# Merging the sums over taps of one chunk with the logits of the next into one run of narrow products

## Chip, cores, metric

One core of a Trainium2 chip. The metric is device time in microseconds, the median of several executions of a whole program.

## The reference, cut to what matters

A token-wise layer norm feeds two branches, and their results are joined as `x + s * silu(b)`.

```python
qkv = (xn @ wqkv) ...            # S = 2048 tokens, D = 512, 32 heads of 16
idx = pos[:, None] - 2 * arange(8)[None, :]           # 8 taps, 2 apart, looking back
logits = einsum("bhsd,bhswd->bhsw", q, k[idx]) * scale
o      = einsum("bhsw,bhswd->bhsd", softmax(logits), v[idx])
s      = o @ wo
b      = (gelu(xn' @ w_gate) * (xn' @ w_up)) @ w_down   # 512 -> 1792 -> 512
```

(In the kernel the second branch uses the same normalized x.) With only eight taps, attention is elementwise work: for each tap VectorE multiplies q by shifted k, and TensorE sums the 16 elements of a head with a matrix of ones that has only 32 columns. The same goes for values. These are the "narrow" products.

Of the kernel before, what the change touches and what calls it, by code (L numbers as in the profile page):

```python
# [8 lines left out]
ALU = mybir.AluOpType  # L9
AF = mybir.ActivationFunctionType  # L10
BF16 = mybir.dt.bfloat16
F32 = mybir.dt.float32

P = 128
H = 32
DH = 16
W = 8
DIL = 2
WL = 4
WH = 2  # L20
PAD = 16
TQ = 512
VW = TQ + WL * DIL
EPS = 1e-5
SCALE = DH ** -0.5
# [3 lines left out]
def kernel(  # L29
# [13 lines left out]
    nc = tc.nc  # L43
    B, S, D = A_x.shape
# [8 lines left out]
    def pool(name, bufs, **kw):  # L53
        return ctx.enter_context(tc.tile_pool(name=name, bufs=bufs, **kw))
# [2 lines left out]
    wts = pool("wts", 1)  # L57
    big = pool("big", 1)
    qp = pool("qp", 1)
    ep = pool("ep", 2)  # L60
    vap = pool("vap", 1)
    prod = pool("prod", 8)
    hp = pool("hp", 16)
    xtp = pool("xtp", 2)
    op = pool("op", 1)
    sm = pool("sm", 3)
    sm2 = pool("sm2", 2)
    sm4 = pool("sm4", 4)
    xnp = pool("xnp", 6)
# [83 lines left out]
            )  # L153

    xnT = {}
    k_sb = big.tile([P, NC, PAD + S], BF16, name="k_sb")
    nc.vector.memset(k_sb[:, :, 0:PAD], 0.0)
    stats = const.tile([P, NT, nc.vector.BN_STATS_DIM], F32, name="stats")
    mv = const.tile([P, NT, nc.vector.BN_AGGR_DIM], F32, name="mv")
    mhalf = const.tile([P, 1], F32, name="mhalf")  # L160
# [87 lines left out]
    def qkv(j, fo, i0=0, n=TQ, ps=None):  # L248
        which, c = divmod(fo, NC)
        if fo == 0 and i0 == 0:  # L250
            st[j]["q"] = qp.tile([P, NC, TQ], BF16, name="q_sb")
        if ps is None:
            ps = mm.tile([P, n], F32, name="qkv_ps", tag="mm")[:]
            project(ps, wqkv_sb, fo * P, j, i0, n)
        if which == 0:
            nc.scalar.activation(out=st[j]["q"][:, c, i0 : i0 + n], in_=ps, func=AF.Copy)  # L256
        elif which == 1:
            lo = PAD + j * TQ + i0
            nc.scalar.activation(out=k_sb[:, c, lo : lo + n], in_=ps, func=AF.Copy)  # L259
        else:  # L260
            vst = sm4.tile([P, TQ], BF16, name="vst")
            nc.scalar.activation(out=vst[:], in_=ps, func=AF.Copy)  # L262
            lo = PAD + j * TQ
            nc.sync.dma_start(out=vT[c * P : (c + 1) * P, lo : lo + TQ], in_=vst[:])

    def load_v(j, wls=range(WL)):

        if wls[0] == 0:
            st[j]["va"] = vap.tile([P, DH, VW], BF16, name="v_arr")
        va = st[j]["va"]  # L270
        for wl in wls:
            nc.sync.dma_start(
                out=va[H * wl : H * (wl + 1), :, :],
                in_=bass.AP(
                    tensor=vT.tensor,
                    offset=PAD + j * TQ - WL * DIL - DIL * wl,
                    ap=[[SV * DH, H], [SV, DH], [1, VW]],
                ),
            )

    def qk_product(j, w):
        pk = prod.tile([P, NC, TQ], BF16, name="pk", tag="prod")
        off = PAD + j * TQ - w * DIL
        nc.vector.tensor_tensor(  # L284
            out=pk[:], in0=st[j]["q"][:], in1=k_sb[:, :, off : off + TQ], op=ALU.mult
        )
        st[j]["pk"][w] = pk

    def logits(j):
        nc.scalar.preload_act_table(AF.Exp)  # L290
        L = att.tile([P, NC, TQ], F32, name="L_ps", tag="quad")
        for wh in range(WH):
            for c in range(NC):
                for wl in range(WL):
                    nc.tensor.matmul(  # L295
                        L[H * wl : H * (wl + 1), wh, :],
                        lhsT=dsum[:, c, :],
                        rhs=st[j]["pk"][WL * wh + wl][:, c, :],
                        start=(c == 0),
                        stop=(c == NC - 1),  # L300
                    )
        E = st[j]["E"] = ep.tile([P, WH, TQ], BF16, name="E")
        nc.scalar.activation(out=E[:], in_=L[:, 0:WH, :], func=AF.Exp, scale=SCALE)
        if j == 0:
            for w in range(1, W):
                wh, wl = divmod(w, WL)
                nc.gpsimd.memset(E[H * wl : H * (wl + 1), wh, 0 : w * DIL], 0.0)

    def denominators(j):

        E = st[j]["E"]
        den = mm.tile([P, P], F32, name="den_ps", tag="mm")
        for wh in range(WH):
            for q in range(4):
                nc.tensor.matmul(  # L315
                    den[H * q : H * (q + 1), :],
                    lhsT=hsum[:],
                    rhs=E[:, wh, q * P : (q + 1) * P],
                    start=(wh == 0),
                    stop=(wh == WH - 1),  # L320
                )
        rs = sm2.tile([P, P], BF16, name="rs")
        with nc.allow_low_precision(reason="as the softmax of the reference"):
            nc.vector.reciprocal(out=rs[:], in_=den[:])
        st[j]["rs"] = rs

    def store_reciprocals(j):
        nc.sync.dma_start(out=rs_d[j][:, :], in_=st[j]["rs"][:])
# [60 lines left out]
    def down(j, tt, cols):  # L389

        n = cols.stop - cols.start
        y = mm.tile([P, n], F32, name="y_ps", tag="mm")
        for fc in range(NF):
            nc.tensor.matmul(  # L394
                y[:],
                lhsT=st[j][fc][:, tt * P : (tt + 1) * P],
                rhs=wd_sb[:, fc, cols],
                start=(fc == 0),
                stop=(fc == NF - 1),
            )  # L400
        sl = sm.tile([P, n], BF16, name="sl")
        nc.scalar.activation(out=sl[:], in_=y[:], func=AF.Silu)  # L402
        return sl

# [21 lines left out]
    def at(key, fn, *args):  # L426
        side.setdefault(key, []).append((fn, args))

    def run(stage, j, i):
        for fn, args in side.get((stage, j, i), ()):  # L430
            fn(*args)

    for i in range(TPQ):
        at(("qkv", 0, i), normalize, TPQ + i)
        at(("glu", 0, 7 + i), moments, 2 * TPQ + i)
        if i < 2:
            at(("glu", 0, i), transpose, TPQ + i)
        at(("glu", 0, 8 + i), normalize, 2 * TPQ + i)
        at(("glu", 1, 0), transpose_by_dma, 2 * TPQ + i)
        at(("glu", 1, 10 + i), moments, 3 * TPQ + i)  # L440
        at(("qkv", 2, 2 * i), normalize, 3 * TPQ + i)
        at(("glu", 2, 0), transpose_by_dma, 3 * TPQ + i)

    for w in range(W):
        at(("glu", 0, w), qk_product, 0, w)
    at(("glu", 0, 9), logits, 0)
    for i in range(8):
        at(("glu", 0, 11 + i) if i < 3 else ("qkv", 1, (0, 1, 2, 4, 5)[i - 3]),
           av_product, 0, i // 2, i % 2)
    at(("qkv", 1, 8), denominators, 0)  # L450
    at(("qkv", 1, 8), av_sums, 0)
    at(("qkv", 1, 8), store_reciprocals, 0)
    at(("qkv", 1, 10), spread_reciprocals, 0)
    at(("down", 0, 0), divide, 0)

    for j in range(1, NJ):
        for w in range(W):
            at(("qkv", j, 9 + w) if w < 3 else ("down", j - 1, w // 3), qk_product, j, w)
        for i in range(TPQ):
            at(("down", j - 1, i), load_v, j, [i])  # L460
        at(("glu", j, 0), logits, j)
        for i in range(8):
            at(("glu", j, 2 + i), av_product, j, i // 2, i % 2)
        at(("glu", j, 11), denominators, j)
        at(("glu", j, 11), av_sums, j)
        at(("glu", j, 11), store_reciprocals, j)
        at(("glu", j, 11), spread_reciprocals, j)
        at(("qkv", j + 1, 6) if j + 1 < NJ else ("down", j, 0), divide, j)


    HT = TPQ // 2
# [41 lines left out]
    for j in range(NJ):  # L513
        for fc in range(NF):
            run("glu", j, fc)
            glu(j, fc)
        if j + 1 < NJ:
            for i in range(12):
                run("qkv", j + 1, i)
                qkv(j + 1, i)  # L520

        todo = []
        for tt in range(TPQ):
            run("down", j, tt)
            last = j * TPQ + tt == NT - 1
            for cols in (slice(0, D // 2), slice(D // 2, D)) if last else (slice(0, D),):
                sl = down(j, tt, cols)
                if todo:
                    finish(*todo.pop())
                if last:  # L530
                    finish(j, tt, cols, sl)
                else:
                    todo.append((j, tt, cols, sl))
        if todo:
            finish(*todo.pop())
# [1 line left out]
_INS = ['A_x', 'A_wqkv', 'A_wo', 'B_x', 'B_w_gate', 'B_w_up', 'B_w_down']  # L537
_OUTS = [((1, 2048, 512), 'bfloat16')]
# [25 lines left out]
```

## The kernel before: what the change and the argument touch

Four chunks j of 512 tokens. For each chunk a gate-and-up stage (`glu`, 14 tiles), the q, k, v projections of the *next* chunk (`qkv`, 12 tiles), and a `down` stage (4 tiles of 128 tokens). Attention is hung into these stages by `at(stage, function)`, which runs the function ahead of that tile.

```python
k_sb = big.tile([P, NC, PAD + S], BF16)          # k of all chunks
prod, hp, ep, vap, att, mm = pools of 8, 16, 2, 1, 1, 4 buffers   # att, mm in PSUM

def qk_product(j, w):                            # one tap, 128 x 2048, VectorE
    nc.vector.tensor_tensor(out=pk, in0=q, in1=k_sb[:, :, off : off + TQ], op=mult)

def logits(j):                                   # narrow: 32 products of 32 columns
    L = att.tile([P, NC, TQ], F32, tag="quad")
    for wh, c, wl: nc.tensor.matmul(L[32*wl : 32*(wl+1), wh], lhsT=dsum[:, c], rhs=pk[4*wh+wl][:, c])
    E = exp(L)                                   # ScalarE, one activation of 1024

def denominators(j): ...                         # narrow: 8 products, then reciprocal on VectorE
def av_sums(j):      ...                         # narrow: 32 products into att "quad"

for j in range(1, NJ):
    qk_product(j, w)  at qkv j, tiles 9 to 11, and down j-1
    load_v(j, part)   at down j-1, one part per tile
    logits(j)         at glu j, tile 0
    av_product(j, .)  at glu j, tiles 2 to 9
    denominators(j), av_sums(j), store and spread reciprocals   at glu j, tile 11
    divide(j)         at qkv j+1, tile 6
# down(tt) and finish(tt - 1), the output product, alternate
```

(Loops written in one line and positions in prose are cuts of this text.)

The softmax here doesn't subtract the row's maximum and nothing guards it: scores larger than these inputs give would overflow.

## Time and profile before

| | before |
|---|---|
| device time, median | 229.72 us (3 runs, 229.64 to 230.14) |
| span of the trace, first to last instruction | 228.0 us |
| TensorE / VectorE / ScalarE busy | 98% / 65% / 57% |
| narrow runs | 8 |

### The profile page before, as it was taken

Reading aid. Unit: us, or ns where it says so; the run is one execution under the profiler, and the core shown is the slowest. Engines: PE = TensorE matmul, PEld = TensorE weight load, DVE = VectorE, ACT = ScalarE, POOL = GpSimd, SP = SyncE. Lnnn points to the kernel's source line nnn. Section 1 sums busy time; section 2 is a strip of 40 time slices with the busy share of each in tenths; the row PEclk is TensorE's granted clock in tenths of the full one; section 3 lists DMA queues with packets and bytes.
Section 4 is the critical chain, followed back from the end, with each engine's and each line's share of the span. In section 5 each row is a group of like instructions: output and inputs, shape, how many; then the busy total and the mean of one; then the engine's idle time right before and its main releaser. Section 6 shows DMA issues by size and latency. Waiting matters only on the chain.

```text
span 228.0 us, 3495 instructions
## 1 busy us (share of the span) xinstructions
PE 222.4 (98%) x1300; PEld 106.8 (47%) x1320; DVE 147.6 (65%) x234; ACT 129.8 (57%) x213; POOL 12.8 (6%) x44
## 2 busy tenths in 40 slices
PE   8999999999999999999999999999999999999993
PEld 6864444444444444444444444444444444444453
DVE  4585996999496298865945369735476429943324
ACT  3779769774423876467621686746642387647210
POOL 1046023100000000110000000000000000000000
PEclk9999999999999999999999999999999999999999
DMA  6999589971399211110287511110149700001011
GB/s 166 354 372 372 146 169 197 247 202 38 101 195 206 70 25 29 26 29 0 92 169 168 139 30 23 26 35 5 39 119 206 169 27 3 0 6 26 0 45 48
DMA packets 31264, 24.62 MB, mean 108 GB/s; under 512 B 10896, under 2 KB 31248, under 8 KB 31248
## 3 DMA queue, kind: packets, MB, share of 16 engines
q1 hardware_dynamic: 31248, 24.41, 42.8%
q8 instruction: 10, 0.16, 0.3%
q14 instruction: 6, 0.05, 0.1%
HBM read 18.74 MB, written 4.34 MB: 101 GB/s over the span
## 4 chain that ended last, share of the span: by engine, by line
PE 95%; ACT 2%; issue 1%; DVE 0%; ACTq 0%; DVEq 0%
PE u_ps L238 21%; PE y_ps L394 21%; PE g_ps L238 19%; PE qkv_ps L238 17%; PE s_ps L410 6%; PE L_ps L295 3%; PE o_ps L357 3%; PE warm_ps L220 2%; PE q_ps L238 1%; ACT u L384 1%; ACT L382 1%; PE tr L203 1%; PE den_ps L315 0%; ACT xnT L212 0%; ACT ge L382 0%
## 5 line engine op out<-in xcount | busy, mean ns | idle before, releaser
L238 PE MATMUL u_ps<-xnT,wu_sb 128*128 128x512 bf16 x224 | 57.5, 379 | 0.3
L238 PE MATMUL g_ps<-xnT,wg_sb 128*128 128x512 bf16 x213 | 56.3, 379 | 0.4
L394 PE MATMUL y_ps<-wd_sb,h 128*128 128x512 bf16 (+1 forms) x236 | 50.2, 366 | 0.1
L386 DVE TENSOR_TENSOR h<-ge,u 128x512 bf16<-128x512 bf16 x56 | 23.7, 424 | 37.0 <-ACT u L384 36.6
L284 DVE TENSOR_TENSOR pk<-q_sb,k_sb 128x2048 bf16<-128x2048 bf16 x32 | 37.5, 1216 | 7.0 <-ACT k_sb L259 7.0
L382 ACT ACTIVATE ge<-g_ps 128x512 bf16<-128x512 f32 x56 | 33.5, 598 | 14.9 <-PE g_ps L238 13.8
L384 ACT ACTIVATE u<-u_ps 128x512 bf16<-128x512 f32 x56 | 33.5, 598 | 14.7 <-PE u_ps L238 14.7
L238 PE MATMUL qkv_ps<-xnT,wqkv_sb 128*128 128x512 bf16 (+1 forms) x203 | 40.5, 354 | 0.3
L343 DVE TENSOR_TENSOR pv<-E,v_arr 128x2048 bf16<-128x2048 bf16 x32 | 38.6, 1218 | 0.2 <-issue 0.2
L394 PEld LDWEIGHTS <-h 128*128 128x128 bf16 x238 | 23.3, 98 | 25.3
L238 PEld LDWEIGHTS <-wu_sb 128*128 128x128 bf16 x224 | 21.9, 98 | 26.6 <-issue 0.3
L238 PEld LDWEIGHTS <-wg_sb 128*128 128x128 bf16 x224 | 21.3, 98 | 27.3 <-issue 3.0
L402 ACT ACTIVATE sl<-y_ps 128x512 bf16<-128x512 f32 (+1 forms) x17 | 9.7, 572 | 41.4 <-PE y_ps L394 39.0
L238 PEld LDWEIGHTS <-wqkv_sb 128*128 128x128 bf16 x224 | 21.8, 98 | 19.8 <-issue 0.4
L418 DVE TENSOR_TENSOR m<-s_ps,sl 128x512 bf16<-128x512 f32 (+1 forms) x17 | 11.2, 657 | 22.2 <-PE s_ps L410 22.2
L410 PE MATMUL s_ps<-wo_sb,oT 128*128 128x512 bf16 (+1 forms) x66 | 15.8, 366 | 0.2
L262 ACT ACTIVATE vst<-qkv_ps 128x512 bf16<-128x512 f32 x16 | 9.6, 598 | 6.5 <-PE qkv_ps L238 6.5
L188 POOL TENSOR_TENSOR rstd<-rstd,mhalf 128x1 f32<-128x1 f32 x12 | 7.7, 640 | 87.4 <-DVE rstd L185 87.4
L259 ACT ACTIVATE k_sb<-qkv_ps 128x512 bf16<-128x512 f32 (+1 forms) x20 | 10.2, 516 | 3.5 <-PE qkv_ps L238 3.2
L369 DVE TENSOR_TENSOR oT<-o_ps,rb 128x1024 bf16<-128x1024 f32 x8 | 9.4, 1216 | 3.1 <-DMA rb<-rs_d 3.1
L256 ACT ACTIVATE q_sb<-qkv_ps 128x512 bf16<-128x512 f32 (+1 forms) x16 | 8.7, 544 | 3.2 <-PE qkv_ps L238 3.0
L410 PEld LDWEIGHTS <-oT 128*128 128x128 bf16 x68 | 6.7, 98 | 7.2
(46 smaller groups left out, 105.9 us busy)
## 6 DMA issues: line engine op xcount, KB each, us to landing
v_arr<-vT SPq DMA_DIRECT2D x16, 520.0 KB, 5.4
vT<-vst SPq DMA_DIRECT2D x16, 128.0 KB, 1.8
out_dram<-o_t SPq DMA_DIRECT2D x15, 128.0 KB, 1.8
wg_sb<-in_B_w_gate_dram SPq DMA_DIRECT2D x2, 896.0 KB, 10.7
wu_sb<-in_B_w_up_dram SPq DMA_DIRECT2D x2, 896.0 KB, 12.3
wd_sb<-in_B_w_down_dram SPq DMA_DIRECT2D x1, 1792.0 KB, 12.3
wqkv_sb<-in_A_wqkv_dram SPq DMA_DIRECT2D x3, 512.0 KB, 5.2
x_sb<-in_A_x_dram SPq DMA_DIRECT2D x3, 512.0 KB, 11.6
```

Of the source, the lines that this page charges most:

```text
L238: nc.tensor.matmul(ps, lhsT=w[:, dk, lo : lo + P], rhs=xnT[j][:, dk, i0 : i0 + n], start=(dk == 0), stop=(dk == NC - 1),)
L259: nc.scalar.activation(out=k_sb[:, c, lo : lo + n], in_=ps, func=AF.Copy)
L262: nc.scalar.activation(out=vst[:], in_=ps, func=AF.Copy)
L284: nc.vector.tensor_tensor(out=pk[:], in0=st[j]["q"][:], in1=k_sb[:, :, off : off + TQ], op=ALU.mult)
L343: nc.vector.tensor_tensor(out=pv[:], in0=st[j]["E"][:, wh, :].unsqueeze(1).to_broadcast([P, 4, TQ]), in1=st[j]["va"][:, 4 * g : 4 * g + 4, ...
L382: nc.scalar.activation(out=ge[:], in_=g_ps[:], func=AF.Gelu_apprx_tanh)
L384: nc.scalar.activation(out=u[:], in_=u_ps[:], func=AF.Copy)
L386: nc.vector.tensor_tensor(out=h[:], in0=ge[:], in1=u[:], op=ALU.mult)
L394: nc.tensor.matmul(y[:], lhsT=st[j][fc][:, tt * P : (tt + 1) * P], rhs=wd_sb[:, fc, cols], start=(fc == 0), stop=(fc == NF - 1),)
L402: nc.scalar.activation(out=sl[:], in_=y[:], func=AF.Silu)
L410: nc.tensor.matmul(s[:], lhsT=st[j]["oT"][:, g, tt * P : (tt + 1) * P], rhs=wo_sb[:, g, cols], start=(g == 0), stop=(g == NC - 1),)
L418: nc.vector.tensor_tensor(out=m[:], in0=s[:], in1=sl[:], op=ALU.mult)
```

## The change

Its intent: sums of chunk j and logits of chunk j+1 use the array in the same narrow form, so put them side by side and switch forms fewer times. For that the products of q and k have to be ready earlier, the logits need other PSUM buffers (they move from the four-bank `quad` to two of the `mm` buffers), and room has to be found in SBUF: k is kept as two chunk buffers with a copied halo (the last 16 columns of the chunk before, to which the taps look back), and four of the eight products lie in v's buffer while v is not loaded. The core of the diff:

```diff
-    prod = pool("prod", 8)
-    hp = pool("hp", 16)
+    prod = pool("prod", 12)
+    hp = pool("hp", 14)
-    k_sb = big.tile([P, NC, PAD + S], BF16, name="k_sb")
+    k_sb = {0: kp.tile([P, NC, PAD + TQ], BF16, name="k_sb")}
...
+    def k_halo(j):
+        k_sb[j] = kp.tile([P, NC, PAD + TQ], BF16, name="k_sb")
+        nc.gpsimd.tensor_copy(out=k_sb[j][:, :, 0:PAD], in_=k_sb[j - 1][:, :, TQ : TQ + PAD])
+
+    def qk_products(j, ws, c0, n):              # n of the 4 column groups, from c0
+        for w in ws:
+            if w not in st[j]["pk"]:
+                if j and w >= WL:
+                    if w == WL:
+                        st[j]["pk4"] = vap.tile([P, WL, NC, TQ], BF16, name="pk4", tag="va")
...
     def logits(j):
+            L = [mm.tile([P, TQ], F32, name="L_ps", tag="mm")[:] for _ in range(WH)]
...
-        at(("glu", 0, 7 + i), moments, 2 * TPQ + i)
+        at(("down", 0, 1), moments, 2 * TPQ + i)
-        at(("glu", 0, 8 + i), normalize, 2 * TPQ + i)
+        at(("down", 0, 2), normalize, 2 * TPQ + i)
...
+    def sums(j):
+        if j + 1 < NJ:
+            nc.scalar.preload_act_table(AF.Exp)
+        denominators(j)
+        av_sums(j)
+        if j + 1 < NJ:
+            logits(j + 1)
+        reciprocals(j)
+        store_reciprocals(j)
+        spread_reciprocals(j)
+        if j + 1 < NJ:
+            load_v(j + 1)
     for j in range(1, NJ):
+        at(("qkv", j, 2), k_halo, j)
+        for i in range(2):
+            at(("qkv", j, 4 + 4 * i), qk_products, j, range(W), 2 * i, 2)
         for i in range(8):
-            at(("glu", j, 2 + i), av_product, j, i // 2, i % 2)
+            at(("glu", j, 3 + i), av_product, j, i // 2, i % 2)
+    at(("glu", NJ - 1, 12), sums, NJ - 1)
...
+            for i, fo in enumerate((0, 1, 4, 5, 2, 3, 6, 7, 8, 9, 10, 11)):
                 run("qkv", j + 1, i)
-                qkv(j + 1, i)
+                qkv(j + 1, fo)
+            for tt in range(TPQ):
+                run("down", j, tt)
+                sl.append(down(j, tt, full))
+                if tt == 0:
+                    sums(j)
+            divide(j)
+            for tt in range(TPQ):
+                finish(j, tt, full, sl[tt])
```

The five value products of chunk 0 that were spread over qkv tiles 0 to 5 are now all asked for at qkv tile 0. The last chunk, which has no next one, keeps its sums in its gate-and-up stage.

More of the change, by code (lines that the diff above doesn't have):

```diff
@@ L59 @@
     qp = pool("qp", 1)
-    ep = pool("ep", 2)
+    kp = pool("kp", 2)
+    ep = pool("ep", 1)
     vap = pool("vap", 1)
-    prod = pool("prod", 8)
-    hp = pool("hp", 16)
+    prod = pool("prod", 12)
+    hp = pool("hp", 14)
     xtp = pool("xtp", 2)
@@ L66 @@
     sm = pool("sm", 3)
+    slp = pool("slp", 4)
     sm2 = pool("sm2", 2)
@@ L155 @@
     xnT = {}
-    k_sb = big.tile([P, NC, PAD + S], BF16, name="k_sb")
-    nc.vector.memset(k_sb[:, :, 0:PAD], 0.0)
+    k_sb = {0: kp.tile([P, NC, PAD + TQ], BF16, name="k_sb")}
+    nc.vector.memset(k_sb[0][:, :, 0:PAD], 0.0)
     stats = const.tile([P, NT, nc.vector.BN_STATS_DIM], F32, name="stats")
@@ L257, in qkv @@
         elif which == 1:
-            lo = PAD + j * TQ + i0
-            nc.scalar.activation(out=k_sb[:, c, lo : lo + n], in_=ps, func=AF.Copy)
+            lo = PAD + i0
+            nc.scalar.activation(out=k_sb[j][:, c, lo : lo + n], in_=ps, func=AF.Copy)
         else:
@@ L268, in load_v @@
         if wls[0] == 0:
-            st[j]["va"] = vap.tile([P, DH, VW], BF16, name="v_arr")
+            st[j]["va"] = vap.tile([P, DH, VW], BF16, name="v_arr", tag="va")
         va = st[j]["va"]
@@ L279, in load_v @@
             )
-    def qk_product(j, w):
-        pk = prod.tile([P, NC, TQ], BF16, name="pk", tag="prod")
-        off = PAD + j * TQ - w * DIL
-        nc.vector.tensor_tensor(
-            out=pk[:], in0=st[j]["q"][:], in1=k_sb[:, :, off : off + TQ], op=ALU.mult
-        )
-        st[j]["pk"][w] = pk
-    def logits(j):
-        nc.scalar.preload_act_table(AF.Exp)
-        L = att.tile([P, NC, TQ], F32, name="L_ps", tag="quad")
+    def k_halo(j):
[7 more added lines that the diff above has]
+                        st[j]["pk4"] = vap.tile([P, WL, NC, TQ], BF16, name="pk4", tag="va")
+                    st[j]["pk"][w] = st[j]["pk4"][:, w - WL]
+                else:
+                    st[j]["pk"][w] = prod.tile([P, NC, TQ], BF16, name="pk", tag="prod")
+            off = PAD - w * DIL
+            nc.vector.tensor_tensor(
+                out=st[j]["pk"][w][:, c0 : c0 + n, :],
+                in0=st[j]["q"][:, c0 : c0 + n, :],
+                in1=k_sb[j][:, c0 : c0 + n, off : off + TQ],
+                op=ALU.mult,
+            )
+    def logits(j):
+        if j == 0:
+            nc.scalar.preload_act_table(AF.Exp)
+            quad = att.tile([P, NC, TQ], F32, name="L_ps", tag="quad")
+            L = [quad[:, wh, :] for wh in range(WH)]
+        else:
+            L = [mm.tile([P, TQ], F32, name="L_ps", tag="mm")[:] for _ in range(WH)]
+        E = st[j]["E"] = ep.tile([P, WH, TQ], BF16, name="E")
         for wh in range(WH):
@@ L295, in logits @@
                     nc.tensor.matmul(
-                        L[H * wl : H * (wl + 1), wh, :],
+                        L[wh][H * wl : H * (wl + 1), :],
                         lhsT=dsum[:, c, :],
@@ L301, in logits @@
                     )
-        E = st[j]["E"] = ep.tile([P, WH, TQ], BF16, name="E")
-        nc.scalar.activation(out=E[:], in_=L[:, 0:WH, :], func=AF.Exp, scale=SCALE)
+        for wh in range(WH):
+            nc.scalar.activation(out=E[:, wh, :], in_=L[wh], func=AF.Exp, scale=SCALE)
         if j == 0:
@@ L321, in denominators, with reciprocals @@
                 )
+        st[j]["den"] = den
+    def reciprocals(j):
+        den = st[j]["den"]
         rs = sm2.tile([P, P], BF16, name="rs")
@@ L400, in down @@
             )
-        sl = sm.tile([P, n], BF16, name="sl")
+        sl = slp.tile([P, n], BF16, name="sl")
         nc.scalar.activation(out=sl[:], in_=y[:], func=AF.Silu)
@@ L434 @@
         at(("qkv", 0, i), normalize, TPQ + i)
-        at(("glu", 0, 7 + i), moments, 2 * TPQ + i)
+        at(("down", 0, 1), moments, 2 * TPQ + i)
         if i < 2:
             at(("glu", 0, i), transpose, TPQ + i)
-        at(("glu", 0, 8 + i), normalize, 2 * TPQ + i)
+        at(("down", 0, 2), normalize, 2 * TPQ + i)
         at(("glu", 1, 0), transpose_by_dma, 2 * TPQ + i)
         at(("glu", 1, 10 + i), moments, 3 * TPQ + i)
-        at(("qkv", 2, 2 * i), normalize, 3 * TPQ + i)
+        at(("qkv", 2, i), normalize, 3 * TPQ + i)
@@ L442 @@
         at(("glu", 2, 0), transpose_by_dma, 3 * TPQ + i)
     for w in range(W):
-        at(("glu", 0, w), qk_product, 0, w)
+        at(("glu", 0, w), qk_products, 0, [w], 0, NC)
     at(("glu", 0, 9), logits, 0)
     for i in range(8):
-        at(("glu", 0, 11 + i) if i < 3 else ("qkv", 1, (0, 1, 2, 4, 5)[i - 3]),
-           av_product, 0, i // 2, i % 2)
-    at(("qkv", 1, 8), denominators, 0)
-    at(("qkv", 1, 8), av_sums, 0)
-    at(("qkv", 1, 8), store_reciprocals, 0)
-    at(("qkv", 1, 10), spread_reciprocals, 0)
@@ L454 @@
-    at(("down", 0, 0), divide, 0)
-    for j in range(1, NJ):
-        for w in range(W):
-            at(("qkv", j, 9 + w) if w < 3 else ("down", j - 1, w // 3), qk_product, j, w)
-        for i in range(TPQ):
-            at(("down", j - 1, i), load_v, j, [i])
-        at(("glu", j, 0), logits, j)
-        for i in range(8):
-            at(("glu", j, 2 + i), av_product, j, i // 2, i % 2)
-        at(("glu", j, 11), denominators, j)
-        at(("glu", j, 11), av_sums, j)
-        at(("glu", j, 11), store_reciprocals, j)
-        at(("glu", j, 11), spread_reciprocals, j)
-        at(("qkv", j + 1, 6) if j + 1 < NJ else ("down", j, 0), divide, j)
+        at(("glu", 0, 11 + i) if i < 3 else ("qkv", 1, 0), av_product, 0, i // 2, i % 2)
@@ new lines, in sums @@
+    def sums(j):
+        if j + 1 < NJ:
+            nc.scalar.preload_act_table(AF.Exp)
+        denominators(j)
[7 more added lines that the diff above has]
+            load_v(j + 1)
+    for j in range(1, NJ):
+        at(("qkv", j, 2), k_halo, j)
+        for i in range(2):
+            at(("qkv", j, 4 + 4 * i), qk_products, j, range(W), 2 * i, 2)
+        for i in range(8):
+            at(("glu", j, 3 + i), av_product, j, i // 2, i % 2)
@@ L517 @@
         if j + 1 < NJ:
-            for i in range(12):
+            for i, fo in enumerate((0, 1, 4, 5, 2, 3, 6, 7, 8, 9, 10, 11)):
                 run("qkv", j + 1, i)
-                qkv(j + 1, i)
-        todo = []
-        for tt in range(TPQ):
-            run("down", j, tt)
-            last = j * TPQ + tt == NT - 1
-            for cols in (slice(0, D // 2), slice(D // 2, D)) if last else (slice(0, D),):
-                sl = down(j, tt, cols)
-                if todo:
-                    finish(*todo.pop())
-                if last:
-                    finish(j, tt, cols, sl)
-                else:
-                    todo.append((j, tt, cols, sl))
-        if todo:
-            finish(*todo.pop())
+                qkv(j + 1, fo)
+            full = slice(0, D)
+            sl = []
+            for tt in range(TPQ):
[6 more added lines that the diff above has]
+                finish(j, tt, full, sl[tt])
+        else:
+            full, half = slice(0, D), (slice(0, D // 2), slice(D // 2, D))
+            sl = [down(j, tt, full) for tt in range(TPQ - 1)]
+            divide(j)
+            finish(j, 0, full, sl[0])
+            finish(j, 1, full, sl[1])
+            sl3 = down(j, 3, half[0])
+            finish(j, 2, full, sl[2])
+            finish(j, 3, half[0], sl3)
+            sl3 = down(j, 3, half[1])
+            finish(j, 3, half[1], sl3)
 _INS = ['A_x', 'A_wqkv', 'A_wo', 'B_x', 'B_w_gate', 'B_w_up', 'B_w_down']
```

## The prediction

> **What bounds the kernel now.** I read the page's busy shares and chain first, then the groups by form of TensorE, then the timelines of TensorE, VectorE and the DMA queue around one chunk boundary.
>
> ```profile
> span 228.0 us, 3495 instructions
> PE 222.4 (98%) x1300; PEld 106.8 (47%) x1320; DVE 147.6 (65%) x234; ACT 129.8 (57%) x213; POOL 12.8 (6%) x44
> ...
> PE 95%; ACT 2%; issue 1%; DVE 0%; ACTq 0%; DVEq 0%
> ```
>
> The chain is TensorE from end to end. A busy 98% could still hide gaps, since matmul ends are modelled, so I counted starts. Four 128x512 products of one projection start every 0.863 us in the timeline, 0.216 us each. From the first up product of chunk 1 (75.31) to that of chunk 2 (129.38) it is 54.07 us. Work in it: 28x4 gate and up, 48 qkv, 56 down, 16 output products, 232 x 0.2158 = 50.07; 64 narrow products, four at once, 16 x 0.2158 = 3.45; eight narrow ones of 128 columns, 0.11. That sums to 53.63. Only 0.44 us of the period is not work: TensorE does not wait for anybody in the middle. What the 0.44 is shows at the edges of a narrow run:
>
> ```profile
> 70.77 1.89 PE L410 MATMUL s_ps<-wo_sb,oT 128*128 128x512 bf16 x8
> 72.59 1.91 PE L295 MATMUL L_ps<-pk,dsum 128*32 128x512 bf16 x32
> 74.43 1.04 PE L238 MATMUL g_ps<-xnT,wg_sb 128*128 128x512 bf16 x3
> ```
>
> The columns are start, length, engine, line, operation. Eight wide products from 70.77 take 1.73 and end their slots at 72.49; the narrow run starts at 72.59. Its 32 products take eight slots, to 74.32; the next wide one starts at 74.43. So entering costs 0.10 us and leaving 0.11 us, 0.21 us a run. Two runs a chunk make the 0.44.
>
> **What the Trainium skill says.** TensorEngine Tiling (Array Packing), section Key Properties: "Changing tiling mode (not just tile) drains the TensorE". The trace agrees: 0.10 us at each edge, and no gap between the denominators and the value sums, both 32 columns wide. TensorE: Matmul & The Clock Gate, section "Wait — 56ns, not 53.3ns?", gives 215.7 ns from start to start for 512 columns warm; the trace has 0.216. The same page, section The mechanism (Part 3), says matmuls start and end in program order, without reordering; so one product that waits for data holds all behind it. No row before shows this, as none waits. ScalarE: Activation LUTs, section What ACT_TABLE_LOAD costs, has 1283 ns for a load plus a drain of about 1380 ns; the trace agrees with 1283 ns, but starts the load within 0.01 us of the activation before it ending, so I count no drain.
>
> **The change, part by part.**
>
> 1. Narrow runs. Before there are eight: logits and sums for each of four chunks. After, in program order, five: logits 0, sums 0 with logits 1, sums 1 with logits 2, sums 2 with logits 3, sums 3. Three runs fewer at 0.21 us: **-0.65 us**, all on the path. TensorE's instruction count is unchanged.
>
> 2. q k products in two halves. A 128x2048 product has a pitch of 1.136 us (five in 5.76 with the last one's tail), a 128x512 one 0.335 (h at 43.58, next at 43.91). The line through both gives 0.60 us for 128x1024, so eight w in two halves take 16 x 0.602 = 9.63 against 9.09: VectorE pays 0.5 us a chunk. It has 35% idle; what counts is when the last half ends against when the merged run wants it. The logits now come about 15 us after the first qkv product; before they came at the end of the down stage, about 28 us after.
>
> 3. That deadline in chunk 1. Here five value products of chunk 0 stand in front:
>
> ```profile
> 42.44 1.22 DVE L343 TENSOR_TENSOR pv<-E,v_arr 128x2048 bf16<-128x2048 bf16 x1
> ...
> 46.85 5.76 DVE L343 TENSOR_TENSOR pv<-E,v_arr 128x2048 bf16<-128x2048 bf16 x5
> 52.53 0.95 DVE L324 RECIPROCAL rs<-den_ps 128x128 bf16<-128x128 f32 x1
> ```
>
> The moments and normalizations that stood in front of these move away, but the fourth load of v lands at 42.06, so the series can start only some 0.3 us earlier, and ends near 52.25. Then the halves: first halves of all eight w to 57.1, second halves of w 0 to 3 to 59.5, of w 4 to 7 to 61.9. TensorE: qkv starts at 44.54 as before; 48 slots to 54.90, one down tile (14 slots) to 57.92, entry 0.10, denominators 0.11, value sums 1.73: logits of w 0 to 3 start at 59.86, in time. Those of w 4 to 7 start at 60.72, their third c group at 61.15, and its w 7 needs the last half, ready at about 62.0. TensorE stops: **+0.9 us**. In chunks 2 and 3 nothing stands in front: k's second column group is there some 4.2 us after the first qkv product, the halves end by 14, and the group that needs the last one comes at 16.6. No stop there.
>
> 4. Transposes by DMA. The sixteen for chunk 2 are issued after the output writes of chunk 0:
>
> ```profile
> 73.08 1.40 SPq L421 DMA_DIRECT2D out_dram<-o_t  x2
> 74.58 21.68 SPq L230 DMA_TRANSPOSE xnT<-xn  x16
> ...
> 128.66 21.10 SPq L230 DMA_TRANSPOSE xnT<-xn  x16
> ```
>
> Issue alone takes 21 us, and the last lands 22.8 us after the first is issued (97.40), 22.2 for chunk 3 (150.87). qkv of chunk 2 started at 100.67, so there was a slack of over 3 us. It goes from both ends. The sums leave the glu stage, so glu to qkv shrinks to 28 x 0.8635 = 24.2 us. And the four output products now come in one piece at the end: m waits 1.13 us after the first one starts, then m and o_t have a pitch of 1.07, so the fourth o_t ends 5.5 us after the first starts, 2.0 after the glu stage has begun; with the write's issue the transposes start at 2.5. The last lands at 2.5 + 22.8 = 25.3; the first projection wants its fourth piece at 24.2 + 0.65 = 24.8: **+0.5 us** for chunk 2. With 22.2 it is 24.7 for chunk 3: nothing.
>
> 5. v's buffer is lent to four products. Its loads can start only after the merged logits, and the queue has reciprocals to store and spread first: for chunk 1 at about 66.3. Four loads in a row took 5.7 us for the first and 14 to the last (issue 27.98, last landed 42.06), so 80.4. The first value product comes after h of the third glu tile, about 6.4 us into the stage, near 81.5. In time, by 1 us; later by 3 or more.
>
> 6. Small things. ScalarE gains a table load a chunk (1.28 us) and eight short activations in place of four long ones; at 57% busy and with waits of about 3 us before each silu, free. GpSimd copies three halos. Divide for chunk 0 ends near 70.4, its first reader comes at 71.7.
>
> Sum: -0.65 + 0.9 + 0.5 = **+0.7 us** on 229.72: **230.4 us**, an increase of 0.3%.
>
> **Rivals.** (a) Only the drains count: both waits fit in slack that I cut too fine. 229.1 us. For it: the two waits are differences of about 1 us between sums of 15 to 25 us, and VectorE's starting point rests on one landing time. Against: both are series of fixed durations, which agree to a few hundredths in all chunks of the trace. (b) The transposes are late in both chunks, or the v loads, now four at once and then output writes in the same rings, push them or the first value products back by 1 to 3 us: 231 to 233 us. For it: in chunk 0 transposes issued behind four v loads landed 11.8 us later. Against: by the time they are issued most of v has landed. (c) VectorE's late series delays the reciprocals, their spreading and so the division: TensorE would wait at the first output product, 1 us or more, 231.5. For it: chunk 0's moments and normalizations, about 5 us, now stand between. Against: my count leaves 1.3 us.
>
> **Range and chances.** All of a merged drain is 0.65 us, and nothing else in the change removes TensorE work, so under 229 is hardly to be had; the low end, 228.9, is rival (a) with run-to-run room. The high end, 231.4, is the sum with one more us of rivals (b) or (c). Two per cent is 4.6 us: faster is out of reach of the mechanism, slower would need several of the waits at once. Faster 0.005, same 0.98, slower 0.015.
>
> **What would show it.** In the timeline of the changed kernel: five narrow runs with 0.1 us at each edge and no gap between value sums and logits within one; a stop of 0.5 to 1.3 us inside the first merged run, before products of pk's last w, put down to VectorE, and none in the two others; a stop of up to 1 us at the first projection of chunk 2, with the sixteenth transpose landing just before it, and less at chunk 3; m and o_t in blocks of four. The chain of waits should have VectorE or DMA pieces at just these two places. I am wrong if TensorE's idle time elsewhere is over 0.5 us, if either stop is absent, or if the period between chunks 2 and 3 does not fall by about 0.2 us.

## More of the kernel before

One more line, of the groups by cost, is used later. It ends with the busy time, the mean of one in ns, and the idle time just before them.

```profile
L343 DVE TENSOR_TENSOR pv<-E,v_arr 128x2048 bf16<-128x2048 bf16 x32 | 38.6, 1218 | 0.2 <-issue 0.2
```

The value products (`pv`) waited for nothing: the loads of v were in time. And TensorE, in the view of waits, waited twice, both at the start of the program:

```profile
PE warm_ps L220 <- PEq L548: 0.8, 1, 0.8
PE q_ps L238 <- ACT xnT L212: 0.2, 1, 0.2
```

## The result, and the profile after

Ratios here and below are the mean time of one kernel's runs over that of the other's in the same rounds, so not quite the ratio of the medians quoted.

| | before | after | ratio, 95% interval |
|---|---|---|---|
| first measurement | 229.73 us (229.47 to 230.14, 6 runs) | 231.25 us (230.57 to 231.99, 6 runs) | 1.0064 [1.0043, 1.0085] |
| again, in a later job | 229.92 us (229.65 to 230.90, 11 runs) | 230.91 us (230.70 to 231.07, 6 runs) | 1.0033 [1.0015, 1.0051] |

The change costs 0.3 to 0.6%. The page's head and the chain's shares by engine:

```profile
span 229.1 us, 3573 instructions
...
PE 223.6 (98%) x1320; PEld 107.0 (47%) x1320; DVE 149.1 (65%) x258; ACT 135.0 (59%) x220; POOL 13.8 (6%) x47
...
PE 71%; DMA 11%; DVE 8%; SPq 7%; issue 1%; DVEq 0%
```

TensorE's busy share is as before, 98%: that number does not tell a wait of one or two microseconds. (1320 against 1300 products is no change; some records were missing from the trace of before.) The chain of work that ended last, followed back from the last instruction, gives a hint (no proof; see late_run): it left TensorE. Followed in order of time (start, length, what), it goes through a load of v and VectorE before it comes back to TensorE in the middle of the first merged run:

```profile
30.20 12.34 DMA v_arr<-vT
...
49.46 3.48 DVE pv L370 x3
52.95 9.65 DVE pk L300 x16
62.59 0.04 issue
62.64 0.59 PE L_ps L318 x5
63.23 9.17 PE y_ps L421 x42
```

The same place in TensorE's timeline, first merged run, chunk 1 (start, length, engine, line, operation; in brackets the idle time before and who ended it):

```profile
57.83 0.29 PE L338 MATMUL den_ps<-E,hsum 128*32 128x128 bf16 x8
57.96 1.90 PE L384 MATMUL o_ps<-pv,hsum 128*32 128x512 bf16 x32
59.68 2.13 PE L318 MATMUL L_ps<-pk,dsum 128*32 128x512 bf16 x26
62.04 0.38 PE L318 MATMUL L_ps<-pk,dsum 128*32 128x512 bf16 x1 [0.23 <-DVE pk L300]
62.64 0.59 PE L318 MATMUL L_ps<-pk,dsum 128*32 128x512 bf16 x5 [0.22 <-DVE pk L300]
63.16 9.24 PE L421 MATMUL y_ps<-wd_sb,h 128*128 128x512 bf16 x42
```

and the same run one chunk later, where nothing waits:

```profile
113.46 0.30 PE L338 MATMUL den_ps<-E,hsum 128*32 128x128 bf16 x8
113.58 1.90 PE L384 MATMUL o_ps<-pv,hsum 128*32 128x512 bf16 x32
115.31 1.90 PE L318 MATMUL L_ps<-pk,dsum 128*32 128x512 bf16 x32
117.14 9.24 PE L421 MATMUL y_ps<-wd_sb,h 128*128 128x512 bf16 x42
```

From the first logit product to the next wide product is 1.83 us without a wait (115.31 to 117.14: eight slots of 0.216 and 0.10 for leaving) and 3.48 us in chunk 1 (59.68 to 63.16). The stop is the difference, **1.65 us**. Beware of the bracketed idle times: they sum to 0.45. Four narrow products lie beside each other, each is drawn 0.38 us long although the next may start after 0.216, and a late one hides in the tail of its neighbours. Stops of a pipelined engine are measured from start to start against an undisturbed copy of the same series, not by adding idle times.

VectorE's timeline tells why the last products came late:

```profile
42.77 1.23 DVE L370 TENSOR_TENSOR pv<-E,v_arr 128x2048 bf16<-128x2048 bf16 x1 [1.90 <-DMA v_arr<-vT]
...
47.19 5.75 DVE L370 TENSOR_TENSOR pv<-E,v_arr 128x2048 bf16<-128x2048 bf16 x5
52.87 9.71 DVE L300 TENSOR_TENSOR pk<-q_sb,k_sb 128x1024 bf16<-128x1024 bf16 x16
62.50 0.95 DVE L351 RECIPROCAL rs<-den_ps 128x128 bf16<-128x128 f32 x1
```

From 42.77 on VectorE has no gap until it delivers the last half product at 62.58. It starts when chunk 0's fourth load of v has landed (42.55 in the trace; in the kernel before, it landed at 42.06, and the first value product began at 42.44, behind a normalization).

The second loss is at the first projection of chunks 2 and 3. An undisturbed qkv stage takes 10.36 us from its first product to the first down product (100.67 to 111.03 before). After:

```profile
99.86 10.64 PE L240 MATMUL qkv_ps<-xnT,wqkv_sb 128*128 128x512 bf16 x48
110.34 3.19 PE L421 MATMUL y_ps<-wd_sb,h 128*128 128x512 bf16 x14
...
153.84 10.71 PE L240 MATMUL qkv_ps<-xnT,wqkv_sb 128*128 128x512 bf16 x48
164.39 3.19 PE L421 MATMUL y_ps<-wd_sb,h 128*128 128x512 bf16 x14
```

10.48 and 10.55 us, so stops of 0.12 and 0.19. The view of waits puts them down on the weight loads, to the transposed x:

```profile
PEld L240 <- DMA xnT<-xn: 0.9, 2, 0.5
```

The DMA queue's timeline has the reason: the output writes come in a block and late, and the transposes stand behind them.

```profile
66.85 2.64 SPq L274 DMA_DIRECT2D v_arr<-vT  x4
74.55 3.51 SPq L448 DMA_DIRECT2D out_dram<-o_t  x4
78.10 21.33 SPq L232 DMA_TRANSPOSE xnT<-xn  x16
```

The last transpose lands at 100.58; the stage that needs it has begun at 99.86.

**The budget.** Measure from the first qkv product of chunk 1 to the first of the last four output products: 44.54 to 223.97 before, 179.43 us; 44.36 to 225.09 after, 180.73 us, so +1.30. Three narrow runs fewer, -0.65 (the predicted figure for their edges); the stop in the merged run, +1.65; the transposes, +0.12 and +0.19. That is +1.31. It leaves 0.01 us for any other change in TensorE's time.

### The profile page after: what moved, and what is told of

Read it like the earlier page. It is cut to its first block, busy times and chain, and to the rows that moved or that the text cites. A ratio compares the mean times of both kernels' runs of the same rounds, so it can differ in the third digit from the quotient of the medians.

```text
span 229.1 us, 3573 instructions
## 1 busy us (share of the span) xinstructions
PE 223.6 (98%) x1320; PEld 107.0 (47%) x1320; DVE 149.1 (65%) x258; ACT 135.0 (59%) x220; POOL 13.8 (6%) x47
## 4 chain that ended last, share of the span: by engine, by line
PE 71%; DMA 11%; DVE 8%; SPq 7%; issue 1%; DVEq 0%
PE y_ps L421 20%; PE g_ps L240 16%; PE u_ps L240 16%; PE qkv_ps L240 9%; PE s_ps L437 6%; DMA x_sb<-in_A_x_dram 5%; DMA v_arr<-vT 5%; DVE pk L300 4%; DVE pv L370 4%; SPq L93 4%; PE o_ps L384 2%; PE L_ps L318 2%; SPq L87 2%; SPq L232 1%; SPq L274 1%
## 5 line engine op out<-in xcount | busy, mean ns | idle before, releaser
L240 PE MATMUL g_ps<-xnT,wg_sb 128*128 128x512 bf16 x224 | 57.5, 379 | 0.0
L300 DVE TENSOR_TENSOR pk<-q_sb,k_sb 128x1024 bf16<-128x1024 bf16 (+1 forms) x56 | 38.9, 760 | 5.0 <-ACT k_sb L261 5.0
L240 PEld LDWEIGHTS <-wu_sb 128*128 128x128 bf16 x224 | 21.9, 98 | 26.6 <-issue 0.3
L437 PE MATMUL s_ps<-wo_sb,oT 128*128 128x512 bf16 (+1 forms) x68 | 14.8, 366 | 0.0
```

The lines of the kernel that those rows point to most:

```text
L240: nc.tensor.matmul(ps, lhsT=w[:, dk, lo : lo + P], rhs=xnT[j][:, dk, i0 : i0 + n], start=(dk == 0), stop=(dk == NC - 1),)
L300: nc.vector.tensor_tensor(out=st[j]["pk"][w][:, c0 : c0 + n, :], in0=st[j]["q"][:, c0 : c0 + n, :], in1=k_sb[j][:, c0 : c0 + n, off : off ...
L437: nc.tensor.matmul(s[:], lhsT=st[j]["oT"][:, g, tt * P : (tt + 1) * P], rhs=wo_sb[:, g, cols], start=(g == 0), stop=(g == NC - 1),)
```

## The experiments

Two theories were put to the test. **Theory A**: the budget above, and within it: the stop is VectorE's saturated series, which begins when v lands and has a deadline set by TensorE's order. **Theory B**: the stops are bookkeeping, and the kernel is slower for something spread out, such as ScalarE's extra table load per chunk, or the output products in blocks. All kernels gave correct results; the first four ran on one chip with eleven runs of before, the other four together with nine.

### after_again: the changed kernel once more

No edit.

> The changed kernel once more, on the chip of the other three. Theory A (a budget of three parts: three narrow runs fewer -0.65 us, one stop of TensorE in the first merged run +1.65, two stops for transposed pieces at the first projections of chunks 2 and 3 +0.12 and +0.19): about 231.2 us, 0.6% above before, and the stop in the first merged run between 1 and 2.2 us, moving with the landing of chunk 0's fourth load of v (42.55 us in the last profile). Because that landing varies, the spread of its times should be wider than that of before, which was 0.7 us over six runs against 1.4. Theory B (the stops are bookkeeping; the kernel is slower because ScalarE swaps tables once more a chunk and the output products come in blocks): the same time, but no relation between stop and span.

Measured: 230.91 us, ratio 1.0033. The stop was 1.38 us, with v landed at 42.20; transposes cost 0.17 and 0.00. Span from first qkv to last output product +0.90 over before, and -0.65 + 1.38 + 0.17 gives 0.90. The stop moved with the landing, as theory A has it: v landed 0.35 us earlier and qkv of chunk 1 began 0.09 earlier than in the first profile, a difference of 0.26, and the stop fell by 0.27. The expectation on the spread was wrong: this kernel's six runs lay within 0.4 us and the eleven of before within 1.25. Whatever varies between executions of before is larger than what v's landing adds.

### late_run: the first merged run one down tile later

```diff
-        at(("down", 0, 1), moments, 2 * TPQ + i)
+        at(("down", 0, 2), moments, 2 * TPQ + i)
-        at(("down", 0, 2), normalize, 2 * TPQ + i)
+        at(("down", 0, 3), normalize, 2 * TPQ + i)
-                if tt == 0:
+                if tt == (1 if j == 0 else 0):
                     sums(j)
```

Moments and normalization move along with the run so that VectorE's order of instructions stays the same; only TensorE's changes.

> The first merged run moved one down tile (3.02 us) later on TensorE; VectorE's order unchanged, everything else the same. Theory A: the last half of the products of w 7 is ready some 1.4 us before it is asked for, so the stop of 1.65 us goes; the division ends close to its first reader, which may cost 0.1. Span 227.5 to 227.7 in place of 229.1, time about 229.7, equal to before within 0.3%, and the spread narrower than that of the changed kernel. Theory B: moving the run by one tile changes neither table loads nor blocks, so the time stays at 231.2.

Measured: 229.72 us against 229.92 for before, ratio 0.9986 [0.9966, 1.0006]; against the changed kernel, 1.2 us gained. The run has no stop:

```profile
60.94 0.29 PE L338 MATMUL den_ps<-E,hsum 128*32 128x128 bf16 x8
61.06 1.90 PE L384 MATMUL o_ps<-pv,hsum 128*32 128x512 bf16 x32
62.79 1.90 PE L318 MATMUL L_ps<-pk,dsum 128*32 128x512 bf16 x32
```

the next wide product starts at 64.62, 1.83 us after 62.79. In this profile the transposes cost nothing either, and the budget is -0.65: TensorE's part is shorter than before by just the drains. Theory B falls: table loads, blocks of output products, activations and halo copies are all still there. The times of this kernel were expected to spread less than those of the changed one; they did not (0.62 us against 0.37). A caution on the chain: this run's page still has DVE at 6% and DMA at 11% on the chain, because its way back leads through products that were ready just in time. A share of the chain is not a stop.

### early_transposes: transposes ahead of the output writes

```diff
-        at(("glu", 1, 0), transpose_by_dma, 2 * TPQ + i)
+        at(("down", 0, 3), transpose_by_dma, 2 * TPQ + i)
-        at(("glu", 2, 0), transpose_by_dma, 3 * TPQ + i)
+        at(("down", 1, 3), transpose_by_dma, 3 * TPQ + i)
```

> Transposes of chunks 2 and 3 issued before the output writes of the preceding chunk rather than after; nothing else. Theory A: the sixteenth lands over 5 us before its first reader, both stops at the first projections go, 0.3 us gained: about 230.9 us. A rival (four loads of v and sixteen transposes in the same rings push each other): v's fourth load lands later than 80.4 and the first value products of chunk 1 wait, or the output writes pile up behind the transposes and VectorE waits for an output buffer; then no gain, or a loss.

Measured: 230.47 us, ratio 1.0020 [0.9998, 1.0042]. Both qkv stages took 10.36 us, so both stops are gone; v's fourth load landed at 80.19, no later than in the changed kernel (80.37). The output writes did pile up, as the rival has it: those of chunk 0 were issued from 92.67 on in place of 74.55. But VectorE waited for no output buffer (the results `o_t` are written from 73.99 on with 0.04 us of idle time before each, as without the edit), so the rival costs nothing. The stop in the merged run stayed, 1.55 us, and the budget closes: -0.65 + 1.55 = 0.90 against 0.89 measured. The expected gain of 0.3 us came out in the time and not in the span, so its size is luck: against the changed kernel of the same rounds the mean time fell by 0.30 us, while the mean span did not fall (228.57 against 228.52; that kernel lost only 0.17 us at the transposes in its profile, and here the other stop was 0.17 longer). The gain lies outside the trace; see below.

### split_runs: the merged runs taken apart again

```diff
-        if j + 1 < NJ:
-            nc.scalar.preload_act_table(AF.Exp)
         denominators(j)
         av_sums(j)
-        if j + 1 < NJ:
-            logits(j + 1)
         reciprocals(j)
...
                 if tt == 0:
                     sums(j)
+                if tt == 1:
+                    next_logits(j + 1)        # table, logits, load_v
```

> The merged runs taken apart again: sums after the first down tile as in the changed kernel, logits of the next chunk after the second one, so three more narrow runs. Theory A: +3 x 0.21 us for the drains, -1.65 us because the first logits are no longer early: span about 228.1, time about 230.2, and 0.4 to 0.65 us slower than the kernel with only the first run moved. If a run costs nothing, it equals that kernel; if theory B holds it is no faster than the changed kernel.

Measured: 230.61 us, ratio 1.0018 [0.9998, 1.0039], 0.9 us over the late run of the same rounds (0.8 by the means), more than the 0.4 to 0.65 expected. One of the added pairs of edges, chunk 2:

```profile
112.45 0.29 PE L338 MATMUL den_ps<-E,hsum 128*32 128x128 bf16 x8
112.58 1.90 PE L384 MATMUL o_ps<-pv,hsum 128*32 128x512 bf16 x32
114.41 3.19 PE L421 MATMUL y_ps<-wd_sb,h 128*128 128x512 bf16 x13
117.53 1.91 PE L318 MATMUL L_ps<-pk,dsum 128*32 128x512 bf16 x32
119.38 1.90 PE L421 MATMUL y_ps<-wd_sb,h 128*128 128x512 bf16 x8
```

Denominators and sums are 0.11 + 1.73 from 112.45 and end at 114.29; the wide product starts 0.12 later. Fourteen slots from 114.41 end at 117.43; the narrow one starts 0.10 later, and after it 0.12 are lost again. So a run costs 0.22 us at its edges, and the three runs are back. The profiled execution is 1.18 us longer than the late run's: those 0.65, and 0.33 and 0.20 us at the transposes, which the late run's profile happened not to lose. The 0.53 is also what its budget shows over before (+0.53, eight runs in both). How much the other executions lost at the transposes is not recorded.

### v_first: chunk 0's v loaded earlier

```diff
-    at(("glu", 0, 0), transpose_by_dma, TPQ + 2)
     at(("glu", 0, 0), load_v, 0)
+    at(("glu", 0, 0), transpose_by_dma, TPQ + 2)
     at(("glu", 0, 0), transpose_by_dma, TPQ + 3)
```

> The changed kernel with chunk 0's loads of v issued ahead of the transposes of tile 6 (which now follow). They wait for v's own writes, landed at 27.5, so they go out about 0.6 us earlier and the last lands near 41.9 in place of 42.2 to 42.55. In three profiles the last half product ended 20.03 to 20.05 us after that landing, and the stop was that end minus the start of qkv of chunk 1 minus 16.57. So the stop should fall by the same 0.3 to 0.6 us, to about 1.0. If the stop has another cause it stays at 1.4 to 1.65. Risk: the transposes of tiles 6 and 7 land later, near 43.3, a little before qkv of chunk 1 wants them at 44.3.

Measured: 229.97 us against 229.95 for before, ratio 1.0006 [0.9993, 1.0019]. The loads of v went out 1.13 us earlier (27.03 in place of 28.16; 0.6 expected) and the last landed at 41.34, not near 41.9, so the stop should fall further than the expected 1.0 us. VectorE's first value product, which waits for the landing, began at 41.46, and VectorE delivered the last half at 61.27, 19.93 us later. By the formula that leaves 61.27 - 44.42 - 16.57 = 0.28 us of stop. Start to start:

```profile
59.74 2.18 PE L318 MATMUL L_ps<-pk,dsum 128*32 128x512 bf16 x32
61.85 9.24 PE L421 MATMUL y_ps<-wd_sb,h 128*128 128x512 bf16 x42
```

2.11 us, less 1.83: 0.28. The size expected was missed, the relation to the landing held. This is the strongest evidence for the cause: a change of order in the DMA queue, 30 us ahead, removes most of the stop, by the number. The transposes of tiles 6 and 7 were in time; no stop shows at qkv of chunk 1.

### whole_products: the halves undone

```diff
-        for i in range(2):
-            at(("qkv", j, 4 + 4 * i), qk_products, j, range(W), 2 * i, 2)
+        at(("qkv", j, 8), qk_products, j, range(W), 0, NC)
```

> The changed kernel with the eight q k products of a chunk undivided, begun when the last column group of k is there; the merged run where the change has it. My step on the halves: they cost VectorE 0.5 us a chunk but begin 3 us earlier. In chunk 1, where VectorE is behind anyway, undivided gives about the same stop (end of the run 0.1 us earlier). In chunks 2 and 3 the last product ends 16.8 us after the first qkv product and is wanted at 16.2 by its first column group: two new stops of about 0.6 us, total 1.0 to 1.2 us more than the changed kernel. A rival (the halves are the cause of the stop in chunk 1) would have this kernel faster.

Measured: 232.19 us against 229.95, ratio 1.0099 [1.0080, 1.0117]. Chunks 2 and 3 now stop too, by 0.81 and 0.76 us; chunk 2:

```profile
115.24 1.25 PE L318 MATMUL L_ps<-pk,dsum 128*32 128x512 bf16 x19
116.92 1.02 PE L318 MATMUL L_ps<-pk,dsum 128*32 128x512 bf16 x13 [0.43 <-DVE pk L300]
117.88 9.24 PE L421 MATMUL y_ps<-wd_sb,h 128*128 128x512 bf16 x42
```

In chunk 1 the stop was 0.76 us in this profile, but there qkv began 0.93 us later than in the changed kernel (45.29 against 44.36, from the start of the program) with v landing at the same time (42.56), which gave VectorE that much more room; less that, 1.69 against 1.65: the same. So the halves cause nothing in chunk 1 and are what keeps chunks 2 and 3 free. (The late start is that of the program: the first load of wqkv held up the first products, before anything that this edit touches. The longer stop that it spared in chunk 1 makes up for it.) Against the changed kernel's first profile the two new stops, 1.57 us (1.2 expected), less 0.29 at the transposes, are the 1.3 us by which the span is longer (230.4 against 229.1).

### late_run_2 and both: the two repairs together

`both` has the edits of late_run and early_transposes.

> The late run again, beside the kernel with both changes and on another chip or day: 0.1 to 0.2% under before, span 0.6 to 0.8 us shorter than before, and time minus span about 2.3 us where before has 1.96. If time minus span is a property of the program it repeats for this kernel and not for the one with early transposes (which had 2.04); if it is chance of the load it does not.

> First merged run one down tile later, and transposes of chunks 2 and 3 ahead of the output writes. Budget theory: from the first qkv product of chunk 1 to the last y half, 0.65 us shorter than before with no stop left anywhere, as the late run alone had it in its one profile (178.78 against 179.43); its profile then had no stop at the transposes by luck of 0.2 us, so the gain over it is 0 to 0.2 us. Span 227.2, time 229.2 to 229.7: at or just under before.

Measured in the same rounds: late_run_2 229.63 us, ratio 0.9989 [0.9976, 1.0001]; both **229.48 us** against 229.95, ratio **0.9979 [0.9965, 0.9992]**, the fastest of all, though only by 0.2%. The late run's profile had a stop of 0.34 us at the transposes of chunk 2 this time; `both` had none, and its budget is -0.66. Its chain is TensorE's again:

```profile
PE 94%; ACT 2%; DVE 1%; DMA 1%; issue 0%; DVEq 0%
```

### The budget over all profiles

All in us, from the first qkv product of chunk 1 to the first of the last four output products, against the 179.43 of before. Drains, the edges of three narrow runs, are set to the predicted -0.65 where runs are merged; the rows without any stop measure it. Each row is one profiled execution; other executions of the same kernel have other landings, and so other stops.

| kernel | drains | stop in merged runs | stops at transposes | sum | measured |
|---|---|---|---|---|---|
| after | -0.65 | 1.65 | 0.12 + 0.19 | 1.31 | 1.30 |
| after_again | -0.65 | 1.38 | 0.17 + 0.00 | 0.90 | 0.90 |
| late_run | -0.65 | 0 | 0 | -0.65 | -0.65 |
| late_run_2 | -0.65 | 0 | 0.34 + 0.00 | -0.31 | -0.31 |
| early_transposes | -0.65 | 1.55 | 0 | 0.90 | 0.89 |
| both | -0.65 | 0 | 0 | -0.65 | -0.66 |
| split_runs | 0 | 0 | 0.33 + 0.20 | 0.53 | 0.53 |
| v_first | -0.65 | 0.28 | 0.00 + 0.01 | -0.36 | -0.36 |
| whole_products | -0.65 | 0.76 + 0.81 + 0.76 | 0.00 + 0.02 | 1.70 | 1.71 |

### What stays open: time outside the trace

Device time is longer than the span from first to last instruction, and not by the same amount. Mean of time minus span over a kernel's runs: before 1.96 and 1.93, early_transposes 2.04, both 2.01, whole_products 1.95; but the changed kernel 2.30 and 2.40, late_run 2.31 and 2.25, split_runs 2.34, v_first 2.27. So there are two levels some 0.35 us apart. A kernel mostly keeps its level (late_run in both of its measurements), but single runs of the changed kernel and of v_first were at 1.97. No record of the trace lies in this time, and what decides the level was not found; the number of instructions does not (the changed kernel, late_run and early_transposes have the same instructions in other orders). It accounts for some 0.35 us of the 1.0 to 1.5 us by which the change is slower, and for most of the difference in time between late_run and both.

## Why the prediction was right, and where it was off

The predicted time, 230.4 us, was below both measurements (231.25 and 230.91), and both lie in the range, the first near its end. The three terms and their places were right; that the sum came near is in part luck, since one wait was set 0.5 to 0.75 us too small and the other 0.2 to 0.3 too large. One of the named signs of being wrong appeared: the period between chunks 2 and 3 (first up product to first up product) was to fall by about 0.2 us. It fell by 0.03 in the first profile (54.08 to 54.05), as 0.19 was lost at chunk 3's transposes, where nothing had been predicted; in after_again, without that stop, it fell by 0.22.

1. *Narrow runs, -0.65 us.* Right: late_run and both are shorter by 0.65 and 0.66. (Three times the 0.21 written there is 0.63; with half of the 0.44 for a run it is 0.66.) Five runs with edges of 0.10 to 0.12 us, and no gap between value sums and logits.
2. *Halves, 0.60 us each.* Right: sixteen took 9.71 us with the tail of the last, 0.60 apart. That chunks 2 and 3 had room was right, and whole_products showed that they have it because of the halves.
3. *The deadline in chunk 1, +0.9 us.* The mechanism was right, and so was the place: the third column group of the last taps, where TensorE waited for the second half of tap 6 and then of tap 7. The term was too small, 1.65 and 1.38 measured, outside the 0.5 to 1.3 given as its sign. In the first profile the difference is the sum of two starting points. The value series ended at 52.87, not 52.25: v landed at 42.55 rather than 42.06, and the first value product began 0.22 after the landing, where I had put 0.09. And TensorE came to the logits at 59.68, not 59.86, since the start of the program was 0.18 shorter. 0.62 + 0.18 is the 0.8 that was missing. I had taken one landing time from one trace as fixed: over the eight traces with this order of loads it lies between 41.99 and 42.56.
4. *Transposes, +0.5 us at chunk 2, nothing at chunk 3.* Right in kind: they were issued 2.4 us into the stage (2.5 predicted). The size was off: 0 to 0.34 us at chunk 2 and 0 to 0.20 at chunk 3 over the profiles of kernels that kept the order. The last transpose landed 22.5 us after the first was issued in place of 22.8, and this varies by more than the slack.
5. *v's loads in its lent buffer, in time by 1 us.* Right: landed 80.37 (80.4 predicted), first used at 82.10. The landing's exactness is luck: the first load was issued at 66.85, not 66.3, and the last landed 13.5 us later, not 14.1. In after_again it landed at 81.13 and was used at 81.75.
6. *Small things, free.* Right: late_run keeps them all and loses nothing. The division ended at 70.98, its first reader came at 72.24.
7. What no step had: 0.35 us outside the trace. The sum of steps holds for the span; the time adds a part that I had taken as constant.

Rival (a), only the drains, is what the kernel became once two lines of order were repaired. Of rival (b) the weak form came true in the first profile, with transposes late in both chunks, but by 0.1 to 0.2 us and not by 1 to 3; that the first time, 231.25, lies in its interval is due to the other stop. Rival (c) did not happen: the division was there 1.26 us before its reader.

## What to carry to other kernels

Where one engine is the bound and never waits, a change that saves it 0.65 us of switching is worth just that, and every input of the series that it moves earlier gets a new deadline: write down, for each, when it is ready and when it is now asked for, from starts in the trace. Do not count on a slack of a few tenths that rests on a DMA landing: here the landing of v moved by 0.6 us between profiles, and that of the last transpose, counted from the first one's issue, by 0.8 (21.9 to 22.7 over kernels that kept the order of the change). Measure a landing in several profiles, or choose an order that leaves more room; here one tile of the down stage gave 3.02 us. Moving the merged run by one tile kept the gain and cost nothing, because the work behind it did not need it earlier.

## What the Trainium skill lacked or had wrong

- TensorEngine Tiling (Array Packing), Key Properties, says that changing the tiling mode drains, but not how much: the runs show 0.10 us into the narrow form and 0.10 to 0.12 us out of it, 0.22 a run.
- ScalarE: Activation LUTs, What ACT_TABLE_LOAD costs, counts a drain of about 1.38 us with each switch. Here a load takes 1.28 us, as the page has it, but no such drain shows on either side: in the changed kernel the load at 18.89 begins 0.02 us after the activation ahead of it has ended, and the next activation begins 0.01 us after the load, 1.31 us for the whole switch.
- DMA: Bandwidth & Descriptors has a bandwidth of DMA transposes in one kernel and a count of sequencer cycles for a large one, but not the pace of a queue of small ones from SBUF to SBUF: sixteen of 128x128 bf16 (32 KB each) go out mostly 1.27 us apart, hold the queue for 21 to 23 us, and land 2.2 us or more after each issue.
- TensorE: Matmul & The Clock Gate says that products keep program order, and the stopped run agrees (the first down product starts at 63.16, behind the last late one); it does not say how a stop looks in a trace when four of them lie side by side. Here a stop of 1.65 us shows 0.45 us of idle time.
- Runtime: NRT & Kernel Launch has a gap between a profile's total time and the reported time that is nearly the same for all kernels; that is another pair of times, and neither this page nor another has the difference of device time and span measured here. It is not the same for all kernels: 1.93 to 2.04 us for four of these and 2.25 to 2.40 us for the others, by a rule not found.
